# The inverse transform's first step taken for two row tiles at a time, with the last 33 columns of both in one product

## The chip, the core and the metric

The kernel runs on one core of a Trainium2 chip. The metric is the device time of a whole execution in microseconds (us). It is measured in rounds, the changed kernel and the kernel before on the same chip. A profile is one traced execution with its own span; the median times come from untraced runs.

Engines are called as the profile calls them: PE is TensorE (PEld its weight loads), DVE is VectorE, ACT is ScalarE, POOL is GpSimd, SP is SyncE, which issues most transfers.

## The reference

The program is the forward and backward pass of a gated mix of two branches: a spectral filter (2-D real FFT, a filter, inverse FFT) and a feed-forward network. Cut to what matters:

```python
g = sigmoid((x * gate_w).sum(-1, keepdims=True))
X = rfft2(x)                       # x: 2048 x 576, so X: 2048 x 289
a = irfft2(X * W)                  # spectral branch
b = (gelu(x @ w_gate) * (x @ w_up)) @ w_down
out = g * a + (1 - g) * b          # and the gradients of all inputs
```

There are two inverse transforms: one for `a`, and one for the gradient of x through the spectral branch. Each has 2048 rows, that is 16 row tiles of 128, and 289 columns l. 289 is 256 + 33, and the 33 are the subject.

## The kernel before

Transforms are products with tables. An inverse goes through a scratch V in DRAM. For each row tile i, a first step z(i) contracts over the rows; its result ZT is transposed, with l on the partitions. A second step d(i) then contracts over l, in three pieces of 128 partitions.

```python
# z(i): three windows of 128 columns of l, at 0, 128 and 161 (L2); the third overlaps the second by 95
for lc, l0 in enumerate((0, P, L2)):
    o = zf[:, lc * 256:(lc + 1) * 256]
    for v in range(2):
        nc.tensor.matmul(o, lhsT=Vp[:, ii, v, l0:l0 + P], rhs=..., start=(v == 0), stop=(v == 1))
zt[i] = unit([6, P], name="ZT")
nc.scalar.copy(zt[i][:]..., zf[:, 0:768])
# d(i): the table of the third window, At2, is zero in its first 95 rows
for c in range(2):
    for lc in range(3):
        nc.tensor.matmul(yps[:, c, :DF], lhsT=Z[:, 2 * lc + c, :],
                         rhs=tb.Dt[lc][:, c, :] if lc < 2 else tb.At2[:, c, :], start=(lc == 0), stop=(lc == 2))
# ... copy, add and subtract, store
# order of the pieces
out = [z(0)]
for i in range(1, T):
    out += [z(i), d(i - 1)]
    if i % 2 == 1 and i + 3 < T:
        out.append(pre(i + 3))
```

These pieces, and those of the middle stage that writes V (`s1`), are put into slots between the feed-forward products, so that PE always has work. All of them and one feed-forward product share one accumulator in PSUM, the memory that PE writes its sums to (the tile `z`, one buffer). PE can start the accumulator's next user only after ACT has copied the last one out.

## Time and profile before

| | before |
|---|---|
| median of 3 runs | 1465.55 us |
| profiled span | 1462.4 us |
| PE busy | 98% of the span, 92% of the chain that ended last |
| first step, 6 products of 256 columns a tile | 0.66 us in the chain |
| second step, 6 products of 289 columns a tile | 0.74 us in the chain |
| copy of ZT, 768 columns | 799 ns |
| DMA share, 580 to 920 us | 44% |

A product's mean duration (273 ns) overlaps its neighbours. What it costs is the distance between starts, and the chain shows that as the length of a group divided by its count. The prediction quotes the lines.

### The profile page before, as it was taken

How to read it: one execution, taken by the hardware profiler on the slowest of the kernel's cores; microseconds unless marked ns; L12 is line 12 of the kernel's file. 1: busy time of each engine (PE TensorE's matmuls, PEld its weight loads, DVE VectorE, ACT ScalarE, POOL GpSimd, SP SyncE). 2: the span in 40 equal slices, each digit the busy share in tenths (PEclk: the TensorE clock that was granted, in tenths of full speed). 3: DMA queues.
4: the chain of work that ended last, by engine and by line, in shares of the span. 5: the costliest groups of instructions: out<-in, count | busy, mean ns of one | idle time of the engine just before them, and what ended most of it. 6: DMA issues, size and time to landing. Idle time of an engine off the chain costs nothing.

```text
span 1462.4 us, 30015 instructions
## 1 busy us (share of the span) xinstructions
PE 1433.0 (98%) x11723; PEld 1068.6 (73%) x11808; DVE 846.0 (58%) x2258; ACT 690.7 (47%) x1355; POOL 118.3 (8%) x203
## 2 busy tenths in 40 slices
PE   7999999999999999999999999999999999999998
PEld 5766777677777677677677677678877777777776
DVE  7697677888887886776776776773000541211100
ACT  5786666766676666666766766662000000000000
POOL 1001011011011001001000000110000100000000
PEclk9999999999999999999999999999999999999999
DMA  5144344455445435334434544657999997878773
GB/s 190 60 127 123 114 126 120 140 146 150 137 132 148 120 117 142 106 110 134 136 104 119 147 126 113 168 135 169 260 195 197 211 205 160 171 157 166 154 149 72
DMA packets 483963, 210.49 MB, mean 144 GB/s; under 512 B 307883, under 2 KB 473932, under 8 KB 483820
## 3 DMA queue, kind: packets, MB, share of 16 engines
q1 hardware_dynamic: 474220, 188.06, 53.6%
q0 software_dynamic: 7792, 19.49, 4.4%
q8 instruction: 92, 1.51, 0.4%
q10 hardware_dynamic: 1808, 1.02, 0.3%
q14 instruction: 51, 0.42, 0.1%
HBM read 40.89 MB, written 93.82 MB: 92 GB/s over the span
## 4 chain that ended last, share of the span: by engine, by line
PE 92%; DVE 3%; issue 1%; ACT 1%; DMA 0%; DVEq 0%; ACTq 0%
PE acc L929 29%; PE wps L443 17%; PE xy L333 16%; PE wps L426 9%; PE z L321 8%; PE wps L456 2%; PE xy L328 2%; PE pf L686 2%; PE z L324 1%; PE pf L674 1%; PE pf L493 1%; PE fx L493 0%; DVE Vt L513 0%; DMA pin<-scr 0%; PE pf L632 0%
## 5 line engine op out<-in xcount | busy, mean ns | idle before, releaser
L929 PEld LDWEIGHTS <-pin 128*128 128x128 bf16 x3456 | 338.0, 98 | 87.1 <-DMA pin<-scr 1.9
L333 PE MATMUL xy<-wgu,xT 128*128 128x512 bf16 x1067 | 257.7, 380 | 9.6 <-issue 7.6
L443 PEld LDWEIGHTS <-xn 128*128 128x128 bf16 x2304 | 225.4, 98 | 32.4 <-issue 0.2
L333 PEld LDWEIGHTS <-xT 128*128 128x128 bf16 x1152 | 106.8, 98 | 137.3 <-issue 29.9
L346 ACT ACTIVATE da<-z,omg 128x256 bf16<-128x256 f32 x288 | 113.2, 474 | 148.0 <-PE z L324 145.0
L946 ACT COPY bo<-acc 128x288 f32<-128x288 f32 x32 | 12.7, 398 | 309.9 <-PE acc L929 251.8
L426 PE MATMUL wps<-dB,A 128*128 128x288 bf16 x1152 | 154.2, 286 | 0.0
L929 PE MATMUL acc<-wd_all,pin 128*128 128x288 bf16 x1152 | 142.8, 286 | 1.6 <-DMA pin<-scr 1.6
L929 PE MATMUL acc<-wgT,pin 128*128 128x288 bf16 x1152 | 143.6, 286 | 0.0
L929 PE MATMUL acc<-wuT,pin 128*128 128x288 bf16 x1152 | 143.6, 286 | 0.0
L321 PE MATMUL z<-wdT,dOT 128*128 128x256 bf16 x1152 | 137.7, 273 | 1.5 <-ACT Y L499 1.2
L426 PEld LDWEIGHTS <-A 128*128 128x128 bf16 x1152 | 112.7, 98 | 35.7
L443 PE MATMUL wps<-dHg,xn 128*128 128x256 bf16 x1152 | 134.4, 273 | 0.0
L443 PE MATMUL wps<-dHu,xn 128*128 128x256 bf16 x1152 | 131.5, 273 | 0.0
L321 PEld LDWEIGHTS <-dOT 128*128 128x128 bf16 x1152 | 111.2, 98 | 18.8 <-issue 5.6
L1003 DVE SCALAR_TENSOR_TENSOR f32t<-gwf,dlog,b16t 128x576 f32<-128x576 f32 x16 | 13.1, 818 | 187.5 <-DMA b16t<-dxa_scr 187.5
L352 ACT ACTIVATE q<-xy 128x512 bf16<-128x512 f32 x144 | 86.0, 597 | 69.6 <-PE xy L333 66.0
L359 DVE TENSOR_SCALAR s<-q 128x512 bf16<-128x512 bf16 x144 | 42.8, 297 | 94.2 <-ACT q L352 92.6
L376 ACT ACTIVATE om<-s 128x512 bf16<-128x512 bf16 x144 | 91.9, 638 | 8.9 <-DVE s L360 8.7
L377 ACT ACTIVATE s<-s 128x512 bf16<-128x512 bf16 x144 | 90.8, 630 | 4.6
L449 POOL DMA_DIRECT2D out_dram<-dw x67 | 48.7, 727 | 540.2 <-ACT dw L404 277.0
L360 DVE TENSOR_TENSOR s<-xb,s 128x512 bf16<-128x512 bf16 x144 | 61.3, 426 | 49.4 <-ACT xb L357 42.8
(182 smaller groups left out, 1807.3 us busy)
## 6 DMA issues: line engine op xcount, KB each, us to landing
scr<-A SPq DMA_DIRECT2D x144, 128.0 KB, 2.1
scr<-dHg SPq DMA_DIRECT2D x144, 128.0 KB, 2.1
scr<-dHu SPq DMA_DIRECT2D x144, 128.0 KB, 2.0
out_dram<-dw POOLq DMA_DIRECT2D x67, 128.0 KB, 2.6
wd_all<-in_B_w_down_dram SPq DMA_DIRECT2D x3, 1728.0 KB, 13.5
out_dram<-dwd POOLq DMA_DIRECT2D x34, 144.0 KB, 2.3
scr_p<-Vt SPq DMA_DIRECT2D x32, 144.5 KB, 2.2
Vp<-scr_p SPq DMA_DIRECT2D x16, 289.0 KB, 3.0
```

Source lines behind the costliest of these rows:

```text
L321: nc.tensor.matmul(zo(t), lhsT=dOT[:, ci, t, :], rhs=wdT[:, ci, :], start=(t % 4 < 2 and ci == 0), stop=False)
L333: nc.tensor.matmul(xy[k][:, t % 2, :], lhsT=xT[:, ci, t, :], rhs=wgu[:, ci, :], start=False, stop=(ci == 3))
L346: nc.scalar.activation(da[:, tt, :], z[:, tt, k, :], ACT.Copy, scale=omg32[:, t:t + 1])
L352: nc.scalar.activation(q[:], xy[:, :, 0:FG], ACT.Square)
L359: V.tensor_scalar(s[:], q[:], A_GELU, 1.0, op0=ALU.mult, op1=ALU.add)
L360: V.tensor_tensor(s[:], xb[:], s[:], op=ALU.mult)
L376: nc.scalar.activation(om[:], s[:], ACT.Sigmoid, scale=-2.0 * C_GELU)
L377: nc.scalar.activation(s[:], s[:], ACT.Sigmoid, scale=2.0 * C_GELU)
L426: nc.tensor.matmul(wps[:, :288], lhsT=tl(0, t)[:, fch * P:(fch + 1) * P], rhs=dB[:, t, h * 288:(h + 1) * 288], start=(t == 0), stop=(t == ...
L443: nc.tensor.matmul(wps[:, cc, :], lhsT=xn[:, t, (c0 + cc) * P:(c0 + cc + 1) * P], rhs=tl(k, t), start=(t == 0), stop=(t == T - 1))
L449: wst[0].dma_start(ov[:, c0:c0 + TPB, fsl], dw[:])
L929: nc.tensor.matmul(acc[:, :288], lhsT=src[:, r, :], rhs=w_of(r)[:, h * 288:(h + 1) * 288], start=(first and r == 0), stop=(last and r == F ...
```

## The change

Two row tiles are taken per first-step piece, with two windows of 128 columns each. The remaining 33 columns of both tiles lie side by side and make one stationary operand (the one that a weight load puts into PE) of 66 columns. V in DRAM is split to suit: a main part of 256 columns and a tail of 33. In the second step the third product has 66 rows, and the table is zero for the 33 of the other tile. The core of the diff (" ..." marks cuts; the new scratches, the loads and the main part's z are left out):

```diff
-                LD.dma_start(dst[i], Vt[:])
+                LD.dma_start(dst[0][i], Vt[:, :, 0:256])
+                LD.dma_start(dst[1][:, i].rearrange("c p l -> p c l"), Vt[:, :, 256:DF])
 ...
-        LD.dma_start(tb.At2[L2NEW:P, :, :], tb.Dt[2][0:DF - 256, :, :])
+        for i in range(2):
+            LD.dma_start(tb.At2[i * NL:(i + 1) * NL, i], tb.Dt[2][0:NL])
 ...
+        def ztail(p):
+                for v in range(2):
+                    nc.tensor.matmul(zps[0:2 * NL, 0, 0:256], lhsT=Vp[:, 1024 + v * 2 * NL:1024 + (v + 1) * 2 * NL],
+                                     rhs=..., start=(v == 0), stop=(v == 1))
+                tails[p] = unit([2, P], name="ZU")
+                nc.scalar.copy(tails[p][0:2 * NL]..., zps[0:2 * NL, 0, 0:256])
 ...
-                    for lc in range(3):
-                        nc.tensor.matmul(yps[:, c, :DF], lhsT=Z[:, 2 * lc + c, :],
-                                         rhs=tb.Dt[lc][:, c, :] if lc < 2 else tb.At2[:, c, :],
-                                         start=(lc == 0), stop=(lc == 2))
+                    for lc in range(2):
+                        nc.tensor.matmul(yps[:, c, :DF], lhsT=Z[:, ii, 2 * lc + c, :], rhs=tb.Dt[lc][:, c, :],
+                                         start=(lc == 0), stop=False)
+                    nc.tensor.matmul(yps[:, c, :DF], lhsT=U[0:2 * NL, c, :], rhs=tb.At2[0:2 * NL, ii, c, :], start=False, stop=True)
 ...
-        out = [z(0)]
-        for i in range(1, T):
-            out += [z(i), d(i - 1)]
-            if i % 2 == 1 and i + 3 < T:
-                out.append(pre(i + 3))
+        out = [z(0), ztail(0)]
+        for p in range(1, T // 2):
+            if p + 1 < T // 2:
+                out.append(pre(2 * p + 2))
+            out += [z(p), d(2 * p - 2), ztail(p), d(2 * p - 1)]
```

More of the change, by code (lines that the diff above doesn't have):

```diff
@@ L40 @@
 LO, HI = slice(0, 64), slice(64, 128)
-L2 = DF - P
-L2NEW = 256 - L2
+NL = DF - 256
 class Unit:
@@ L201 @@
     scr_g = dram.tile([T, P, 2, DF], BF16, name="scr_g")
-    scr_p1 = dram.tile([T, P, 2, DF], BF16, name="scr_p1")
-    scr_p2 = dram.tile([T, P, 2, DF], BF16, name="scr_p2")
+    scr_p1 = (dram.tile([T, P, 2, 256], BF16, name="scr_p1"), dram.tile([2, T, P, NL], BF16, name="scr_q1"))
+    scr_p2 = (dram.tile([T, P, 2, 256], BF16, name="scr_p2"), dram.tile([2, T, P, NL], BF16, name="scr_q2"))
     xn = res.tile([P, T, D], BF16, name="xn")
@@ L269 @@
     tb.Rt = []
-    tb.At2 = hres.tile([P, 2, DF], BF16, name="At2")
+    tb.At2 = hres.tile([P, 2, 2, DF], BF16, name="At2")
     hctr = [0]
@@ L660, in f @@
             def f():
-                vp[i0] = load_V(s, i0)
+                Vp = vp[i0] = unit([4 * DF], name="Vp")
+                LD.dma_start(Vp[:, 0:1024].rearrange("p (i n) -> p i n", i=2),
+                             s[0][:].rearrange("t (j i) c l -> (t j) i (c l)", i=16)[:, i0:i0 + 2, :])
+                LD.dma_start(Vp[:, 1024:].rearrange("p (c n) -> p c n", c=2),
+                             s[1][:].rearrange("c t (j q e) l -> (t j) q c (e l)", q=8, e=2)[:, i0 // 2])
             f.noslot = True
@@ L663, in pre, with z @@
             return f
-        def z(i):
+        tails = {}
+        def z(p):
             def f():
-                Vp = vp[i // 2 * 2]
-                ii = i % 2
+                Vp = vp[2 * p]
                 zps = pftile()
-                zf = zps[:].rearrange("p a b -> p (a b)")
-                for lc, l0 in enumerate((0, P, L2)):
-                    o = zf[:, lc * 256:(lc + 1) * 256]
-                    for v in range(2):
-                        nc.tensor.matmul(o, lhsT=Vp[:, ii, v, l0:l0 + P],
-                                         rhs=tb.B[:, 1 - v:3 - v, :].rearrange("q v m -> q (v m)"), start=(v == 0), stop=(v == 1))
-                zt[i] = unit([6, P], name="ZT")
-                nc.scalar.copy(zt[i][:].rearrange("p a m -> p (a m)"), zf[:, 0:768])
+                for ii in range(2):
+                    for lc in range(2):
+                        for v in range(2):
+                            l0 = ii * 512 + v * 256 + lc * P
+                            nc.tensor.matmul(zps[:, ii, lc * 256:(lc + 1) * 256], lhsT=Vp[:, l0:l0 + P],
+                                             rhs=tb.B[:, 1 - v:3 - v, :].rearrange("q v m -> q (v m)"),
+                                             start=(v == 0), stop=(v == 1))
+                zt[p] = unit([2, 4, P], name="ZT")
+                nc.scalar.copy(zt[p][:].rearrange("p i a m -> p i (a m)"), zps[:])
+            return f
@@ new lines, in ztail, with f @@
+        def ztail(p):
+            def f():
+                zps = pftile()
+                Vp = vp.pop(2 * p)
+                for v in range(2):
+                    nc.tensor.matmul(zps[0:2 * NL, 0, 0:256], lhsT=Vp[:, 1024 + v * 2 * NL:1024 + (v + 1) * 2 * NL],
+                                     rhs=tb.B[:, 1 - v:3 - v, :].rearrange("q v m -> q (v m)"), start=(v == 0), stop=(v == 1))
+                tails[p] = unit([2, P], name="ZU")
+                nc.scalar.copy(tails[p][0:2 * NL].rearrange("p a m -> p (a m)"), zps[0:2 * NL, 0, 0:256])
@@ L681, in f @@
             def f():
-                Z = zt.pop(i)
+                ii = i % 2
+                Z, U = zt[i // 2], tails[i // 2]
                 yps = pftile()
                 for c in range(2):
-                    for lc in range(3):
-                        nc.tensor.matmul(yps[:, c, :DF], lhsT=Z[:, 2 * lc + c, :],
-                                         rhs=tb.Dt[lc][:, c, :] if lc < 2 else tb.At2[:, c, :],
-                                         start=(lc == 0), stop=(lc == 2))
+                    for lc in range(2):
+                        nc.tensor.matmul(yps[:, c, :DF], lhsT=Z[:, ii, 2 * lc + c, :], rhs=tb.Dt[lc][:, c, :],
+                                         start=(lc == 0), stop=False)
+                    nc.tensor.matmul(yps[:, c, :DF], lhsT=U[0:2 * NL, c, :], rhs=tb.At2[0:2 * NL, ii, c, :], start=False, stop=True)
                 ev = unit([2, DF], F32, name="ev")
@@ L695, in d @@
             return f
-        out = [z(0)]
-        for i in range(1, T):
-            out += [z(i), d(i - 1)]
-            if i % 2 == 1 and i + 3 < T:
-                out.append(pre(i + 3))
-        return out + [d(T - 1)], [pre(0), pre(2)]
+        out = [z(0), ztail(0)]
[3 more added lines that the diff above has]
+            out += [z(p), d(2 * p - 2), ztail(p), d(2 * p - 1)]
+        return out + [d(T - 2), d(T - 1)], [pre(0), pre(2)]
     def head_tile():
```

## The prediction

> **What bounds the kernel now.** I read the head of the page first, for the share of each engine; then the chain of work that ended last; then the groups of the inverse stage, which is all that the change touches.
>
> ```profile
> span 1462.4 us, 30015 instructions
> ...
> PE 1433.0 (98%) x11723; PEld 1068.6 (73%) x11808; DVE 846.0 (58%) x2258; ACT 690.7 (47%) x1355; POOL 118.3 (8%) x203
> ...
> PE 92%; DVE 3%; issue 1%; ACT 1%; DMA 0%; DVEq 0%; ACTq 0%
> ```
>
> TensorE (PE) is busy for 98% of the span and carries 92% of the chain. Nothing else is near it. So a change is worth the TensorE time that it removes, less the new waits that it gives TensorE, and little else counts.
>
> The inverse transforms run from about 579 to 914 us, as pieces put into slots between the feed-forward products. Over 580 to 920 us the busy time by engine is:
>
> ```profile
> 580.00:920.00 340.00, 336.51 (x2707) 244.52 (x2737) 244.12 (x675) 230.39 (x446) 31.46 (x49) 1.00 0.44 122
> ```
>
> The columns are PE, weight loads, DVE, ACT, POOL, granted clock, DMA share, GB/s. PE is busy for 336.5 of 340 us at full clock and the DMA engines 44%. The list of PE's waits names no DMA and no ScalarE copy in this window; its largest entry, 2.9 us, is "issue" ahead of the feed-forward product. The pieces themselves, by shape (count | busy, mean ns of one | idle before):
>
> ```profile
> L674 PE MATMUL pf<-Btab,Vp 128*128 128x256 bf16 x192 | 26.2, 273 | 0.0
> L677 ACT CAST ZT<-pf 128x768 bf16<-128x768 f32 x32 | 25.6, 799 | 3.6 <-PE pf L674 2.8
> L686 PE MATMUL pf<-Dt,ZT 128*128 128x289 bf16 x128 | 25.0, 287 | 0.0
> L691 ACT ACTIVATE ev<-pf 128x578 f32<-128x578 f32 x32 | 20.9, 652 | 5.9 <-PE pf L686 4.3
> L686 PE MATMUL pf<-At,ZT 128*128 128x289 bf16 x64 | 18.3, 286 | 0.0
> ```
>
> The mean of 273 ns is not what a product costs TensorE: it overlaps its neighbours. The cost on the path is in the chain, in order of time (start, length, what):
>
> ```profile
> 581.91 0.66 PE pf L674 x6
> 582.56 1.96 PE wps L426 x16
> 584.52 1.75 PE z L321 x16
> 586.27 0.33 PE z L324 x4
> 586.59 0.43 PE xy L328 x4
> 587.02 0.16 issue
> ...
> 588.86 0.74 PE pf L686 x6
> ...
> 605.88 1.96 PE wps L426 x16
> 607.84 0.83 PE pf L686 x6
> ```
>
> Six products of 256 columns (the first step, L674) take 0.66 us, 109 ns each; 16 of the same width at L321 take 1.75 us, again 109. Six of 289 columns (the second step, L686) take 0.74 us, 123 each. The last line shows one piece at 0.83: it had waited 0.09 us for its accumulator.
>
> **What the Trainium skill says.** "TensorE: Matmul & The Clock Gate", section "Back-to-back issue gap": N/2.4 + 2.5 ns per isolated product, which is 109.2 for N=256 and 122.9 for 289. The trace agrees (109, 123). The same section's lower sustained rates do not show here. The same page, "LDWEIGHTS (loading the stationary operand)": the time follows the number of columns, not of rows, so 66 rows save nothing in the last product of the second step. "TensorEngine Tiling (Array Packing)", "Key Properties": changing the tiling mode drains the engine. The trace shows a cost of that kind around the 64-row products above: L324 takes 0.33 us for two side-by-side pairs that would need 2 x 0.109 = 0.22, and 0.16 us of "issue" follows L328, so 0.27 us for going in and out. "DMA: Bandwidth & Descriptors", "Specifications": below 512 B a transfer is not at line rate. No line before isolates that for this scratch.
>
> **The change part by part.** There are two inverses of 16 row tiles, so 16 pairs.
>
> *First step.* Before, l is cut into three windows of 128 (0, 128, 161), the last overlapping the second by 95 columns, because only 33 are new. A tile costs 3 x 2 = 6 products, a pair 12. After, a pair has 2 tiles x 2 windows x 2 = 8, and the two 33s sit side by side as a stationary operand of 66 columns for 2 more: 10. Saved: 2 x 16 = 32 products of 256 columns, 32 x 0.109 = **3.5 us**, all on the path. This is the point of the change.
>
> *Second step.* Still 6 products of 289 columns a tile. The third has 66 rows, half of them against zeros in the table: 32 x 2 x 0.123 us before and after. No gain, no loss.
>
> *Weight loads.* The tail's 66 columns are loaded 32 times. The 64-column loads at L456 take 106 to 110 ns against 98 for full ones; if that holds for 66 columns and about 10 ns are not hidden, 32 x 0.01 = 0.3 us at most. I count 0.1.
>
> *ScalarE.* From 578 to 768 columns a copy goes from 641 to 799 ns, 0.83 ns a column. A copy of 1024 is then 799 + 256 x 0.83 = 1.01 us, and one of 256 columns 799 - 512 x 0.83 = 0.37. A pair goes from 1.60 to 1.38 us, 3.5 us less in all. ScalarE is 68% busy there and not the bound, so this is worth nothing directly.
>
> *The shared accumulator.* All pieces and the feed-forward's z use one accumulator tile, so TensorE can start the next user only after the copy. Following the pieces in the timeline from copy to next user, usually 0.5 to 2.8 us is to spare, but some have 0.05 to 0.2. The piece of 581.91 is copied until 584.21 (ScalarE was busy with other work first), and the next user starts at 584.36. Four of the 32 first-step pieces are that tight. Half of the 32 become long ones (0.21 us more copy), half short ones (0.43 less). So about two of the four can stall, 2 x 0.21 = **0.4 us**; the 0.09 at 607.84 may go. Net 0.3.
>
> *Slots.* 32 per inverse before (16 + 16), 32 after (8 + 8 + 16), so their places in the feed-forward stage do not move.
>
> *Transfers.* Written: 32 tiles, each 128 runs of 1156 B before; after, 256 runs of 512 B and 256 of 66 B. Read: 16 pairs, each 128 runs of 2312 B before; after, 128 of 2048 B and 256 of 132 B. If every run is a packet, 32 x 384 + 16 x 256 = 16384 more. The page's queue q1 took 53.6% of 16 engines' span for 474220 packets, 26 ns each, so the addition is 16384 x 26 / 16 = 27 us of all 16 engines, spread over 600 us that are under half full. The issues:
>
> ```profile
> scr_p<-Vt SPq DMA_DIRECT2D x32, 144.5 KB, 2.2
> Vp<-scr_p SPq DMA_DIRECT2D x16, 289.0 KB, 3.0
> ```
>
> A load lands in 3.0 us and is used four or five slots later, each about 5 us apart (64 slots in 335 us). Before too, a pair was loaded some five slots ahead, so the new order of loads changes no wait. SyncE issues 48 more transfers at about 0.4 us; it waits far longer than that for others' data. Off the path.
>
> Sum: 1465.55 - 3.5 + 0.1 + 0.3 = **1462.4 us**, 0.2% less. The last third (from 1030 us, TensorE again nearly full) only starts earlier.
>
> **Rivals.**
> 1. *The 66-row or 66-column product counts as another mode and drains TensorE.* For: 64-row products do so in this trace, 0.27 us in and out. Against: 66 doesn't fit a half array, so it should run in the full one. If it were so: 64 third products in the second step and 16 tail pairs in the first, 80 x 0.27 = 22 us, giving 1484 us, 1.3% slower. I give it 6%.
> 2. *The longer copy holds the accumulator and the gain goes into waits.* For: the tight pieces above. Against: the median piece has over 1 us. To cancel 3.5 us all 16 long pieces would have to wait their full 0.21 (3.4 us); then about 1465.5. 10%.
> 3. *The small runs delay loads or the SyncE queue, and a store or weight load behind them comes late.* For: four times the runs per store. Against: DMA at 44 to 47% there, and no DMA among PE's waits in the window. If a few loads slipped, 1463 to 1468.
> 4. *No stalls, and the removed tight pieces give back a little:* 1461.8.
>
> **Range and chances.** The centre is the count of products, which is sure, with a small loss. The low end is the full 3.5 us plus the runs' own spread of about 1 us each way; the high end is rival 2 with a little noise. Range 1460.4 to 1465.2. A gain of 2% would need 29 us, eight times what is removed; a loss of 2% needs rival 1 and more. Faster 0.003, same 0.987, slower 0.01.
>
> **What will show it.** In the changed profile, the first step should have 128 + 32 = 160 products for the 192, at 109 ns apart, with the 66-column weight loads near 110 ns. The copies should be 16 of about 1.01 us and 16 of about 0.37. PE busy should be about 3 us lower in the inverse stage, with the clock still 1.00. The second step should stay at 0.74 us a piece in the chain; 1.2 or more would be rival 1. PE's waits should gain under 1 us of waits for ScalarE copies (3 us: rival 2) and none for DMA (any: rival 3). I am wrong if the time does not fall by 2 to 4 us, or if it falls by more, which would mean a wait that I took for harmless was on the path.

## More of the kernel before

Tiles called `unit` (Vp, ZT, ev, yo, Vt and others) come from one pool of 19 buffers.

## The result

| | before | changed |
|---|---|---|
| median, same rounds (6 runs each) | 1465.84 us (1463.18 to 1466.31) | 1461.78 us (1460.27 to 1463.87) |
| ratio, 95% interval | | 0.9977 (0.9964 to 0.9990) |
| profiled span | 1462.4 us | 1460.1 us |

A ratio is the mean time of one kernel's runs over that of the other's of the same rounds, so it is not quite the ratio of the two medians. Later, on a chip where the kernel before took 1469.6 us, the changed kernel had 0.9968 (0.9956 to 0.9981). Predicted were 1462.4 us and a range of 1460.4 to 1465.2.

The head of the page of the changed kernel, and its share of the chain by engine:

```profile
span 1460.1 us, 29983 instructions
...
PE 1429.2 (98%) x11691; PEld 1065.0 (73%) x11776; DVE 846.9 (58%) x2258; ACT 686.8 (47%) x1355; POOL 119.1 (8%) x203
...
PE 91%; DVE 4%; issue 1%; ACT 1%; DMA 0%; DVEq 0%; ACTq 0%
```

PE has 32 instructions fewer (11723 to 11691) and is 3.8 us less busy. ACT is 3.9 us less busy, which is worth nothing by itself as ACT is not the bound. PE is the bound as before.

The groups of the inverse stage by shape, in the changed kernel (busy us, mean ns of one | idle before):

```profile
L681 PE MATMUL pf<-Btab,Vp 128*128 128x256 bf16 x128 | 16.6, 273 | 0.0
L694 PE MATMUL pf<-Btab,Vp 128*66 128x256 bf16 x32 | 6.1, 273 | 0.0
L709 PE MATMUL pf<-At,ZU 66*128 66x289 bf16 x64 | 18.4, 288 | 0.0
L685 ACT CAST ZT<-pf 128x1024 bf16<-128x1024 f32 x16 | 16.2, 1013 | 4.2 <-PE pf L681 3.6 <-DMA scr<-dHu 0.3 <-DMA scr<-A 0.3
L697 ACT CAST ZU<-pf 66x256 bf16<-66x256 f32 x16 | 5.8, 363 | 0.1
L694 PEld LDWEIGHTS <-Vp 128*66 128x66 bf16 x32 | 3.5, 111 | 1.9
```

There are 128 + 32 = 160 first-step products for 192. None of the groups has PE idle before it. (Rows overlap: one of 273 ns still runs when the next product is due 109 ns after its start, so a wait under about 0.16 us does not show as idle, and a longer one shows that much too short.) In the chain of the changed kernel (start, length, what):

```profile
602.34 0.22 PE pf L694 x2
...
605.27 0.25 PE pf L707 x2
605.51 0.12 PE pf L709
605.64 0.25 PE pf L707 x2
605.89 0.12 PE pf L709
606.01 1.96 PE wps L425 x16
607.98 0.87 PE pf L681 x8
```

Eight products of the main part take 0.87 us and two of the tail 0.22, 109 ns each. The second step takes 0.74 us, as before, and its 66-row product is no longer than the others, to 0.01 us.

**Where the time went, by stage.** The feed-forward's first product (writing `z`) comes 72 times, at the same places of both programs, and serves as a clock. The 41st comes before the first inverse piece, the 67th after the last. First before, then changed (start, length):

```profile
571.53 1.91 PE L321 MATMUL z<-wdT,dOT 128*128 128x256 bf16 x16
...
927.61 1.91 PE L321 MATMUL z<-wdT,dOT 128*128 128x256 bf16 x16
```

```profile
572.10 1.91 PE L320 MATMUL z<-wdT,dOT 128*128 128x256 bf16 x16
...
924.99 1.91 PE L320 MATMUL z<-wdT,dOT 128*128 128x256 bf16 x16
```

The inverse stage took 927.61 - 571.53 = 356.08 us before and 924.99 - 572.10 = 352.89 us after, **3.19 us less**. In a second profile of the changed kernel it was 352.89 again. The rest of the program did not get shorter. The changed kernel came to the stage 0.57 us later: it was 0.37 us ahead at its first such product, near 53 us, lost 0.91 us in one feed-forward step near 300 us, and was equal to within 0.03 us in all others. After the stage it took 0.31 us more. So -0.37 + 0.91 + 0.03 - 3.19 + 0.31 = -2.3 us, which is the difference of the profiled spans.

**The 0.91 us near 300 us.** The timeline of the changed kernel at that place:

```profile
303.04 0.41 SPq L613 DMA_DIRECT2D out_dram<-o  x1
307.58 0.64 ACT L637 CAST Vt<-pf 128x578 bf16<-128x578 f32 x1 [3.06 <-PE wps L442]
308.27 1.91 PE L320 MATMUL z<-wdT,dOT 128*128 128x256 bf16 x16 [0.75 <-ACT Vt L637]
```

PE waited 0.75 us for the accumulator, because ACT's copy to Vt came late. The bracket puts ACT's wait down to a PE product, but that had long been done. In the trace, the store issued at 303.04 landed at 307.44, and the copy started 0.14 us later. Before, the same store landed at 306.86 and the copy started at 306.96. The copy needs one of the 19 buffers, and by these times the one that it gets is that of the tile `o`, which the store reads. No line of the changed kernel's profile names the buffer; the waits of the kernel before do name the store (ACT's copy to Vt for the store of `o`: 2.1 us, once). Is that loss the change's doing? Experiments e4, e7, e9 and e10 ask this.

### The profile page after: what moved, and what is told of

Read it like the earlier page. It is cut to its first block, busy times and chain, and to the rows that moved or that the text cites. A ratio compares the mean times of both kernels' runs of the same rounds, so it can differ in the third digit from the quotient of the medians.

```text
span 1460.1 us, 29983 instructions
## 1 busy us (share of the span) xinstructions
PE 1429.2 (98%) x11691; PEld 1065.0 (73%) x11776; DVE 846.9 (58%) x2258; ACT 686.8 (47%) x1355; POOL 119.1 (8%) x203
## 3 DMA queue, kind: packets, MB, share of 16 engines
q1 hardware_dynamic: 491416, 188.10, 54.3%
## 4 chain that ended last, share of the span: by engine, by line
PE 91%; DVE 4%; issue 1%; ACT 1%; DMA 0%; DVEq 0%; ACTq 0%
PE acc L950 29%; PE wps L442 17%; PE xy L332 16%; PE wps L425 9%; PE z L320 8%; PE wps L455 2%; PE xy L327 2%; PE z L323 1%; PE pf L707 1%; PE pf L681 1%; PE pf L492 1%; PE pf L709 1%; PE fx L492 0%; DVE Vt L512 0%; DMA pin<-scr 0%
## 5 line engine op out<-in xcount | busy, mean ns | idle before, releaser
L425 PE MATMUL wps<-dB,A 128*128 128x288 bf16 x1152 | 154.2, 286 | 0.0
L425 PEld LDWEIGHTS <-A 128*128 128x128 bf16 x1152 | 112.7, 98 | 35.7
```

What stands on the lines that cost most here:

```text
L425: nc.tensor.matmul(wps[:, :288], lhsT=tl(0, t)[:, fch * P:(fch + 1) * P], rhs=dB[:, t, h * 288:(h + 1) * 288], start=(t == 0), stop=(t == ...
```

## The experiments

There were nine runs, in three calls: seven further kernels, one of them (one store of V) twice, and the changed kernel again. All gave right results. The chips of these were slower for every kernel (before: 1468.9 to 1469.6 us median), so ratios are compared, and the inverse stage in the profiles by the clock above.

### e1: the tail products twice

```diff
-                for v in range(2):
+                for v in (0, 1, 0, 1):
                     nc.tensor.matmul(zps[0:2 * NL, 0, 0:256], ...
```

> The changed kernel with the two tail products of every pair issued twice (32 products of 256 columns more; the result stays right), so 12 first-step products a pair as before the change, and everything else as changed. Theory (the gain is the 32 products): 32 x 0.109 = 3.5 us more than the changed kernel, so the ratio to the kernel before goes from 0.9977 to about 1.000, and the inverse stage in the profile grows by 3.5 us. Rival (the gain comes from the shorter copies or the new loads and scratch): the ratio stays near 0.998.

Measured: 1468.51 us median (5 runs), ratio 1.0001 (0.9988 to 1.0013). The stage's two ends in its profile:

```profile
571.85 1.91 PE L320 MATMUL z<-wdT,dOT 128*128 128x256 bf16 x16
...
928.14 1.91 PE L320 MATMUL z<-wdT,dOT 128*128 128x256 bf16 x16
```

The stage took 356.29 us, 3.40 more than the changed kernel's and 0.21 more than before's. With the 32 products back, the gain is gone, although the new copies, loads, scratch and order are all still there. So the gain is the product count, and the rest of the change costs about 0.2 us in this stage.

### e3: the two tails apart

```diff
-                    nc.tensor.matmul(zps[0:2 * NL, 0, 0:256], lhsT=Vp[:, 1024 + v * 2 * NL:1024 + (v + 1) * 2 * NL], ...
+                    for e in range(2):
+                        c0 = 1024 + (2 * v + e) * NL
+                        nc.tensor.matmul(zps[64 * e:64 * e + NL, 0, 0:256], lhsT=Vp[:, c0:c0 + NL], ...
 # the copy in two parts; table and third product likewise at partitions 0 to 32 and 64 to 96
-                    nc.tensor.matmul(yps[:, c, :DF], lhsT=U[0:2 * NL, c, :], rhs=tb.At2[0:2 * NL, ii, c, :], ...
+                    nc.tensor.matmul(yps[:, c, :DF], lhsT=U[64 * ii:64 * ii + NL, c, :], rhs=tb.At2[64 * ii:64 * ii + NL, ii, c, :], ...
```

> The changed kernel with the 33 columns of the two tiles not in one product: each tile's 33 are a stationary operand of their own, in its own half of the array's columns, and the third product of the second step has 33 rows in a half of the rows. Result right. The first-step tails then run side by side in pairs and cost no more array time (16 pairs of pairs at about 0.054 us each). Theory that narrow shapes cost a change of mode, as the 64-row and 64-column products of the feed-forward do in the trace of before (about 0.2 us into and out of 64 columns, 0.27 us of 64 rows): 16 x 0.2 + 64 x 0.27 = 20 us more than the changed kernel, ratio about 1.012. Rival that only the count of products matters: no change, 0.998. In the chain a second-step piece should go from 0.74 to about 1.3 us.

Measured: 1481.45 us (4 runs), ratio 1.0082 (1.0067 to 1.0098). The chain in its profile:

```profile
602.71 0.33 PE pf L696 x4
...
605.85 0.25 PE pf L710 x2
606.10 0.23 PE pf L712
606.33 0.35 PE pf L710 x2
606.68 0.23 PE pf L712
606.91 2.07 PE wps L425 x16
```

A second-step piece takes 0.25 + 0.23 + 0.35 + 0.23 = 1.06 us for 0.74. The group after it takes 2.07 us where the same 16 products take 1.96. The tail piece takes 0.33 us for 0.22. The stage took 369.69 us, 16.8 more than the changed kernel's. By the parts: 32 x 0.32 + 16 x 0.11 + (32 + 16) x 0.11 = 17.3. The rival that only products count falls. Narrow products cost extra where they alternate with full ones. The size was below the expected 20 us: a 33-row product cost (0.32 + 0.11) / 2 = 0.21 us in and out (0.20 by the starts: 220 ns after a full product and 226 to the next, where the 66-row one has 124 and 126), not the 0.27 read off the kernel before.

That 0.27 was a misreading. Of it, 0.16 us was the "issue" after L328. There one record is missing: the chain shows 7 products of L333 for 8, and the first comes 535 ns after the 64-row product before it, which is 308 and one more product. The trace of before has 1067 of 1152 such records; in the profiles of e6 to e10 all 1152 are there, the "issue" is gone and the distance is 308 to 319 ns. Full products of that width start 216 ns apart, so going out of 64 rows costs about 0.09 us. Going in costs 205 - 109 = 96 ns. Together that is 0.19 us, and (64 + 16) x 0.2 = 16 us would have been the better expectation.

"Both in one product" is thus not only a saving of products: 66 columns and 66 rows do not pay what 33 pay.

### e5: the long copy twice

```diff
-                nc.scalar.copy(zt[p][:].rearrange("p i a m -> p i (a m)"), zps[:])
+                for _ in range(2):
+                    nc.scalar.copy(zt[p][:].rearrange("p i a m -> p i (a m)"), zps[:])
```

> The changed kernel with the long copy of the first step (1024 columns, 1.01 us) made twice, so that the shared accumulator is held 1.01 us longer 16 times. Result right. From the changed kernel's profile, the time between the end of that copy and the accumulator's next user is under 1.1 us in 8 of the 16 cases; with about 0.1 us of it needed anyway, the waits would add up to 0.59 + 0.59 + 0.57 + 0.60 + 0.96 + 0.96 + 0.98 + 0.38 = 5.6 us. Theory (the single accumulator makes a longer copy cost what exceeds the room behind it): 5 to 7 us more, ratio about 1.0015. Rival (ScalarE has room, copies are hidden): under 1 us more. Second rival (every copy on the path): 16 us more, ratio 1.009.

Measured: 1470.71 us (4 runs), ratio 1.0012 (0.9998 to 1.0026). The stage took 359.26 us, 6.4 more than the changed kernel's. New among PE's waits (us in total, times, longest):

```profile
PE pf L708 <- ACT ZT L686: 2.0, 4, 1.0
PE z L320 <- ACT ZT L686: 2.0, 3, 0.8
```

These sum to less than 6.4 us, as the list cuts 0.16 us off each wait. The first theory holds, 5 to 7 us against the 16 us of added copying. A copy on an engine that is not the bound costs what exceeds the room behind it, and that room could be read off the timeline.

### e6: a pair loaded one slot ahead

```diff
-            if p + 1 < T // 2:
-                out.append(pre(2 * p + 2))
-            out += [z(p), d(2 * p - 2), ztail(p), d(2 * p - 1)]
+            out += [z(p), d(2 * p - 2), ztail(p)]
+            if p + 1 < T // 2:
+                out.append(pre(2 * p + 2))
+            out += [d(2 * p - 1)]
```

> The changed kernel with each later load of a pair issued one slot before the pair is used, not four. Result right. A load lands in 3.0 us and a slot is about 5 us, but the load also waits in SyncE's queue behind stores that wait for VectorE (up to 10 us in the list of waits of before). Theory (the load is needed only some slots later and the early issue is what keeps it hidden): some of the 14 loads come late, 2 to 20 us more than the changed kernel. Rival (one slot is enough, the order of loads plays no part in the result): the same within 0.5 us, ratio 0.9977.

Measured: 1472.05 us (5 runs), ratio 1.0025 (1.0011 to 1.0038). The stage took 360.43 us, 7.5 more. PE's waits now name the load:

```profile
PE pf L681 <- DMA Vp<-scr_p: 5.4, 3, 2.9
```

Three of the loads came late, 5.4 us together by this list. By the starts there are four such waits, with 6.2 us. The other 1.3 us followed the longest wait, 2.9 us: the granted clock over 845.0 to 848.5 us was 0.58, products started 213 ns apart in place of 109, and the eight of the first-step piece took 1.89 us for 0.87. The rival falls: the lead of a pair is needed. It adds nothing over before, which had the same lead.

### e7: the kernel before with the added transfers

```diff
                 LD.dma_start(dst[i], Vt[:])
+                LD.dma_start(scr_q[id(dst)][:, i].rearrange("c p l -> p c l"), Vt[:, :, 256:DF])
 ...
                 vp[i0] = load_V(s, i0)
+                LD.dma_start(spare[:]..., scr_q[id(s)][:]...[:, i0 // 2])
```

> The kernel before, with its products, and with small transfers added as the change adds them: for each of the 32 V tiles a tail store of 256 runs of 66 B into a scratch of its own, and for each of the 16 pairs a load of 256 runs of 132 B into a spare tile that nobody reads. Result right. Theory (these transfers are off the path): the kernel before within 0.5 us, ratio 1.000. Rival (they cost the changed kernel part of its gain): 0.9 us or more slower than before, ratio 1.0006 or more, with new waits in the profile between 200 and 580 us.

Measured: 1469.34 us (5 runs), ratio 1.0002 (0.9990 to 1.0015). Its inverse stage was 356.08 us, as before's. By the clock, it lost 0.50 us in the step that ends near 308 us (see e4), and 1.27 us in the one that ends at 280 us. There the added store is named:

```profile
279.94 0.64 ACT L639 CAST Vt<-pf 128x578 bf16<-128x578 f32 x1 [1.38 <-DMA scr_q<-Vt]
280.63 1.91 PE L323 MATMUL z<-wdT,dOT 128*128 128x256 bf16 x16 [1.10 <-ACT Vt L639]
```

The tail store landed at 279.84 and the copy into the buffer that it had read started at 279.94. So the tail stores can reach the path, as the rival says. The timed runs do not show the cost: 1.0002, with an interval that has both theories in it. What is settled is that the added loads cost nothing in the inverse stage.

### e4, and again e9: one store of V, cut at the load

```diff
-                LD.dma_start(dst[0][i], Vt[:, :, 0:256])
-                LD.dma_start(dst[1][:, i].rearrange("c p l -> p c l"), Vt[:, :, 256:DF])
+                LD.dma_start(dst[i], Vt[:])
 # pre: three loads, Vp[:, 0:1024] <- V[.., 0:256], and for each tile Vp[:, 1024:] <- V[.., 256:DF]
```

> The changed kernel with V stored whole, in one transfer of 1156 B runs as before the change, and cut into main and tail at the load (3 transfers a pair, runs of 512 B and 66 B). Result right. Theory (the split store is off the path; the 0.9 us that the changed kernel lost once near 300 us of the profile, where a copy waited for an earlier store to land, is a DMA that happened to land late): the same time as the changed kernel within 0.5 us, ratio 0.9977, and the loss near 300 us may come or not. Rival (the split stores cost SyncE issue time and DMA packets, and the 0.9 us are theirs): 0.9 us or more faster, ratio 0.997, and no loss near 300 us in its profile.

Measured: 1464.71 us (5 runs), ratio 0.9968 (0.9955 to 0.9980). That looked better than 0.9977. It was run at another time. So it ran again, beside the changed kernel.

> The changed kernel itself again, as the control of this call. 0.9977 of the kernel before within 0.0013. In its profile the inverse stage should be 3.2 us shorter than before's, to 0.1 us; the one wait near 300 us, 0.9 us in its first profile, may have any size from 0 to 2 us if it is the landing of a store that varies (the six experiments so far had 0.4 to 1.7 there).

> One store of V again (e4_one_store), beside the changed kernel on the same chip. Theory (split or whole store is off the path): the same as the changed kernel of this call within 0.0010. Rival (the whole store saves something): 0.0006 or more below it, in ratio.

Measured: changed kernel 1464.64 us, ratio 0.9968 (0.9956 to 0.9981); one store 1464.74 us, 0.9970 (0.9957 to 0.9982). They are the same in time. The inverse stage took 352.89 us in all the profiles of both. The split costs SP time, though. Here are the issues of a V tile (ns, least/median/most), before and then changed:

```profile
L638 SPq DMA_DIRECT2D scr_p<-Vt x32: 319/339/442, 267.0 to 567.6; - x32
```

```profile
L638 SPq DMA_DIRECT2D scr_p<-Vt x32: 524/564/630, 266.7 to 568.5; - x32
L639 SPq DMA_DIRECT2D scr_q<-Vt x32: 592/602/614, 267.4 to 569.1; - x32
```

Two feed-forward steps of the middle stage turned out to vary between profiles of one program. The one that ends near 308 us, 14.55 us long before, was 0.91 and 0.28 us longer in the two profiles of the changed kernel, 1.30 and 1.10 with one store, 0.71 in e3, 1.73 in e5, 0.46 in e6, 0.50 in e7, and not at all in e1, which splits the store. (The expectation of e8 counts all six; e1's 0.37 us was in the other step.) So that loss is not the split store's. It need not be the change's either: up to 540 us the kernel with one store issues what the kernel before issues, but for the larger table At2 and its one more transfer near 52 us, and it lost more than the changed kernel.

The one that ends near 280 us, where e7 lost 1.27, was 0.28 longer in the second profile of the changed kernel and 0.37 in e1, each time after a copy that waited 0.4 to 0.5 us for a tail store; it was not longer in the first profile of the changed kernel, in e3, e5 or e6, nor in the two with one store. This small loss comes with the split, now and then. In all ten profiles other than e10's the copy to Vt near 307 us started 0.10 to 0.15 us after the landing of the store of `o`, which took 3.6 us in the kernel before and 3.8 to 4.8 in the others. The kernel before sits just short of that wait: its copy ended at 307.60 and the accumulator's next user started at 307.71. With only one profile of it, whether the change makes this wait likelier stays open.

### e10: the store of `o` issued first

```diff
                     LD.dma_start(o3v[:, i0:i0 + 2, :], o[:, :, 1, :])
-                stores.append(store)
+                stores.insert(0, store)
```

> The changed kernel with the stores of the two filter gradients put at the front of the list of waiting stores, so that they are issued ahead of the transposed weight loads and not behind them. Result right. Theory (the wait near 300 us is ScalarE's copy to Vt waiting for a buffer that the filter gradient's store still reads; that store sat behind two transposes of 2.2 and 1.3 us on SyncE): the store is issued about 3 us earlier and the wait is gone; the feed-forward step in which it falls is 0 to 0.1 us longer than before's, and the time is about 0.9 us less than the changed kernel's, ratio about 0.997. Rival (another buffer or transfer ends that wait): the wait stays, same ratio.

Measured: 1468.53 us (5 runs), ratio 0.9995 (0.9981 to 1.0008), 4 us slower than the changed kernel. This attempt failed, and its profile says why. First SP's own waits, then ACT's, from 260 us on:

```profile
SPq L612 <- DVE o L599: 19.7, 2, 14.2
```

```profile
ACT Vt L637 <- DMA scr_q<-Vt: 3.9, 1, 3.9
```

SP takes its transfers in order. At the head of the list the store of `o` waited up to 14.2 us for DVE to make `o`, and the stores of A and V behind it waited too. A copy to Vt then waited 3.9 us for a V store, and PE 3.6 us for the copy. After that the granted clock was 0.51 over 283.5 to 287.0 us, and 16 products of z took 3.46 us for 1.84, another 1.6 us lost. The list had the store at its end for a reason. At the place near 308 us, though, the theory held. The stores of `o` were issued at 303.69 and 304.15 us, while PE was by then 5.3 us behind the changed kernel: the second came 6.0 us after the feed-forward step's start, in place of 10.2. The copy then waited for nothing, and the step took 14.55 us, as before. Part of that lead came from PE's own stall, so this is no fix. No version that beats the changed kernel was found.

## Why the prediction was right

**What bounds the kernel**: right. PE carries the chain before and after, and its busy time in the inverse stage fell from 352.4 to 349.4 us, by the 3 us expected.

**The whole**: the centre lay 0.6 us above the measured median, and the stage shortened by 3.19 us for a forecast of 3.1. The prediction also called itself wrong if the time fell by more than 4 us. By the medians it fell 4.06 us, and 4.97 later; by the ratios 3.4 (1.5 to 5.3) and 4.7 (2.8 to 6.5). So the timed runs alone do not tell 3.1 from 4 or 5; what says that no further wait was removed in the inverse stage is its length, 352.89 us in both profiles.

**First step, 32 products, 3.5 us**: right. The count fell by 32, the distance stayed 109 ns, and e1, which puts the 32 back, gave back 3.40 us of the stage.

**Second step, no gain and no loss**: nearly. By the starts in the trace, a product after a 66-row one comes 126 to 127 ns later, where one after the third product of before came 122.5 to 123.3 ns later. The other two distances nearly cancel (122.8 to 124.5, and 125.0 to 123.6). Over 64 such products that is some 0.2 us, which the prediction had as nothing.

**Weight loads, 0.1 us**: off by that much. The 66-column load takes 111 ns, as reckoned from 64 columns, but the tail products stand 109.1 ns apart, so nothing of it showed. The 66-row loads took 97 ns for 98 of 128 rows: as expected, fewer rows save nothing.

**ScalarE copies**: 1.01 and 0.37 us expected, 1013 and 363 ns measured, worth nothing directly, as said.

**The shared accumulator, 0.3 us net**: right in kind, smaller in size. In the second-step pieces that follow the L425 group, the distance to the product before has a mean of 149.7 ns over 7 pieces, where the products need 122.5; that is 0.19 us of waits. Before it was 133.9 over 8, 0.09 us. So the net is 0.1. e5 shows that the mechanism is there, and how steep it gets when the copy grows by a microsecond. With the second step's 0.2 the net of the stage comes to -3.5 + 0.2 + 0.1 = -3.2, the 3.19 measured. The prediction had -3.1 with the small terms placed otherwise.

**Transfers off the path**: right in the inverse stage and for the time, not quite in the middle stage, where a tail store's landing now and then held a copy, and PE for about 0.3 us (1.3 in e7). Two sizes were off. SP needs 0.56 + 0.60 us for a V tile's stores in place of 0.34, 0.83 more, not 0.4. The page counts 17,198 more packets, not 16,384; and the queue's share rose from 53.6% to 54.3%, which is about 0.007 x 1460 = 10 us of the 16 engines, not 27: some 9 ns for each added packet, where the prediction took the mean of all, 26.

**The last third only starts earlier**: right to 0.3 us in the first profile. Later the part after the stage took 2.5 to 5.6 us longer than in before's profile, e7 with before's products too (4.2), so those spans are not compared.

**Rival 1**, the mode change: e3 shows what it would have cost, 16.8 us, and the changed kernel that 66 rows and columns do not pay it. The prediction's 0.27 us a product was a misreading (see e3), so its 22 us should have been 16. The largest of PE's waits that it names, 2.9 us of "issue", is of the same kind: missing records, and no wait. **Rival 2**, the gain lost in accumulator waits: not so, by the two figures above. **Rival 3**, late transfers: no DMA among PE's waits in the inverse stage; e6 shows what that would look like. **Rival 4**, no stalls and a little given back: not so either, as the waits grew by 0.1 us; that its 1461.8 us is the measured median is luck.

## What to carry to other kernels

When one engine carries nearly the whole chain, count the instructions that a change takes off it, at the distance between their starts and not at their mean duration, and subtract only the waits that you can point to. Remainders of a tiling (here 33 of 289) are worth packing together, so long as the packed operand stays in the shape of its neighbours. A regular group that both programs share is a good clock: it shows to 0.1 us in which stage the time changed, where spans of single profiles differ by more for other causes. Before a small idle time of PE is read as a cost, count the records around it: where one is missing, its time looks like a wait.

## What the Trainium skill lacked or had wrong

- "TensorE: Matmul & The Clock Gate", "LDWEIGHTS (loading the stationary operand)": it gives columns / 1.2 ns, 55 for 66 columns. The profile rows show 98 ns for 128 columns, 111 for 66, and 96 for 33 in e3 (in another mode), so a row's duration does not follow the columns.
- "TensorEngine Tiling (Array Packing)", "Key Properties": it says that a change of mode drains the engine, with no figure. Here a 33-row product between full ones cost 0.20 us more, in and out (e3), and the 64-row products of the feed-forward 0.19. That 66 rows (124 to 127 ns from start to start for 289 columns) and 66 columns (109 ns for 256) cost no such change is not said either.
- "DMA: Bandwidth & Descriptors": it has no figure on how SP's issue time grows with the number of runs (contiguous pieces). A store of 128 runs of 1156 B took 339 ns to issue, one of 256 runs of 512 B 564, one of 256 runs of 66 B 602.
